# DeltaNet recurrence on Trainium2: five products as single heads in 64x64 tiles in place of stacked pairs of heads

## The chip, the cores and the metric

The kernel runs on one core of a Trainium2 chip. The metric is the device time of one execution in microseconds (us). Three runs of the kernel before took 383.0, 385.54 and 389.6 us; the median is 385.54. One execution more was taken with the hardware profiler.

## The reference

Two blocks follow one another. The first is a DeltaNet recurrence over 4 batches of 8 heads (32 heads in all), 768 tokens and a head dimension of 48. Cut to what matters:

```
k_n = k / (norm(k) + 1e-06)
for t in range(S):
    y[:, :, t] = einsum('bhd,bhde->bhe', q[:, :, t], state)
    v_old = einsum('bhde,bhd->bhe', state, kt)
    state = state + bt * einsum('bhd,bhe->bhde', kt, vt - v_old)
```

The output of the token comes from the state before the token's own update. The second block routes the 3,072 tokens (rows of 384 = 8 heads x 48) to one of 8 experts each by the largest logit, keeps the 80 tokens with the largest gate weight per expert, and runs a two-layer network (384 to 1,024 to 384, ReLU) on them. All other rows of the output are zero.

## The kernel before, in words

The recurrence is done in 12 chunks of 64 tokens. Inside a chunk the step-by-step update becomes matrix algebra: a unit triangular matrix of 64x64 per head is inverted, and products with it, with K, with Q and with the state S (48x48 per head) do the rest. A loop over `j` runs one stage per chunk. In stage j the chain for chunk j runs beside the preparation of later chunks.

All 32 heads are handled in each step. A head has three coordinates: `e` and `p` (0 or 1) and `g` (0 to 7). On chip, tensors with 64 rows per head hold two heads on 128 partitions, and which coordinate picks the half of the partitions depends on the tensor. All of this is in float32.

The products of stage j in TensorE's order are:

- `chain_ks`: K S, the state read with the chunk's keys, into the PSUM tile `a`. VectorE then forms R = V - K S.
- `logits` of chunk j-1 (24 small matmuls).
- `merge_f` of chunk j+1: the block B1 of the triangular matrix times the inverted 16x16 diagonal blocks that ScalarE has placed in `XB` (`place_x`). VectorE copies the result into `FB` under a mask.
- `chain_tr`: the inverse times R, into the tile `m2`. VectorE scales it by gam into `UB`.
- `chain_qs`: Q S, into `a`.
- `merge_y` of chunk j+1.
- `chain_ku`: K U, added into the state in PSUM, `S_ps`. ScalarE copies the state into `SB`.
- `chain_pu`: P U, added into `a` on top of Q S. ScalarE copies this output out (`x_out`), and a DMA writes it to `x_rows`.
- `merge_p` and `merge_u` of chunk j+1 in 32x32 tiles, with two Gram products of chunk j+5 between (`gram`), then transposes of the output (`out_t`).

Five of these (`chain_ks`, `chain_qs`, `chain_ku`, `chain_pu`, `merge_f`) take two heads in one matmul: two heads lie on the two halves of the 128 contraction rows, and the right side (`SB`, `UB`, `XB`) is stored block by block, with each head's data in one half of the columns and zeros in the other. So a product is 16 matmuls with 96 columns. `chain_tr` and `gram` instead take one head per matmul, on tiles of the array of 64 rows by 64 columns; the helper `tiles` deals the 32 matmuls out over four quadrants in turn. A helper `mm` records every matmul, so they all have line L231 in the profile.

The order of the work is written out by hand: each engine runs its instructions in the order in which the code emits them, and waits on semaphores for operands. The DMAs of the loop are issued by SP, also in order: `store` of B1 in eight small pieces, `load_v`, `fetch`, `load_kq`, in even stages `put` and `spread` (the inverted blocks, which POOL has solved, go out to memory and come back in another layout as XD and YD), `load_k`, zeroing of the output (`clear`), early weights (`load_first`), and `x_rows`. `fill` puts small VectorE steps of the gate between. From stage 7 on (`late`) there is no Gram product left, and `merge_p` comes ahead of `chain_pu`.

After stage 11 come the last gate steps, the choice of the 80 tokens, and the experts' network, which the change doesn't touch.

Of the kernel before, what the change touches and what calls it, by code (L numbers as in the profile page):

```python
# [32 lines left out]
def _layout(inputs):  # L33
# [13 lines left out]
    out["vtok"] = vb.transpose(4, 0, 5, 3, 1, 2, 6).reshape(NC, 128, 16 * D)  # L47
# [30 lines left out]
def kernel(  # L78
# [89 lines left out]
    with ExitStack() as actx:  # L168
# [19 lines left out]
        XB = blk.tile([128, NB, 2, 48], F32, name="XB")  # L188
        YB = blk.tile([128, NB, 2, 2, 16], F32, name="YB")
        FB = blk.tile([128, 2, 4, 2, 64], F32, name="FB")  # L190
        YF = fixed("YF", 2, [128, 2, 8, 64])
        PB_ = blk.tile([128, 2, 8, 32], F32, name="PB")
        SB = blk.tile([128, NQ, 2, 2, D], F32, name="SB")
        UB = blk.tile([128, NB, 2, D], F32, name="UB")
# [21 lines left out]
        PAIRS = [(a, 4 * c + ql) for a in range(2) for ql in range(4) for c in range(2)]  # L216
        XPAIRS = [(a, 4 * c + 2 * r + q) for a in range(2) for c in range(2) for q in range(2) for r in range(2)]

# [11 lines left out]
        def mm(out, lhsT, rhs, acc=False):  # L230
            nc.tensor.matmul(out, lhsT=lhsT, rhs=rhs, start=not acc, stop=not acc, skip_group_check=True)  # L231

# [51 lines left out]
        def norm_of(bs, ss):  # L284
# [22 lines left out]
            for i, c in enumerate(bs):  # L307
                for e in range(2):
                    for h in range(2):
                        nc.gpsimd.tensor_copy(nvs[hs(h), c, 8 * e : 8 * e + 8].rearrange("r (q p) -> r p q", p=2),  # L310
                                              nv[hs(e), i, :, h].rearrange("r (p q) -> r p q", p=2))
# [89 lines left out]
        def place_x(c, es=(0, 1)):  # L401
            if ok(c):
                for e in es:
                    for i in range(3):
                        nc.scalar.mul(XB[hs(e), :, e, 16 * i : 16 * i + 16], XD[hs(e), :, c % 2], bmask[hs(e), i : i + 1])  # L405

# [8 lines left out]
        def merge_f(c, ps):  # L415
            if ok(c):
                for p, g in PAIRS:
                    mm(ps[hs(g // 4), p, 96 * (g % 4) : 96 * (g % 4) + 96].rearrange("r (e w) -> r e w", e=2),
                       B1[c % B1n][:, slot(p, g)], XB[:, slot(p, g)])
                for p in range(2):  # L420
                    nc.vector.copy_predicated(FB[:, p].rearrange("r g e w -> r (g e) w")[:, :, 0:48],  # L421
                                              mask48.bitcast(I32).unsqueeze(1).to_broadcast([128, 8, 48]),
                                              ps[:, p, :384].rearrange("r (g w) -> r g w", w=48))

        def merge_y(c, ps):
            if ok(c):
                for m in range(8):
                    for e in range(2):
                        mm(ps[hs(e), 0, 64 * m : 64 * m + 64], FB[:, m // 4, m % 4, e], YB[:, 8 * e + m].rearrange("r h b w -> r (h b w)"))
# [5 lines left out]
        def merge_p(c, ps, eng=None):  # L435
            if ok(c):
                for m in range(8):
                    for e in range(2):
                        for h in range(2):
                            k = 64 * h + 32 * (m % 2)  # L440
                            mm(ps[k : k + 32, 1, 128 * e + 32 * (m // 2) : 128 * e + 32 * (m // 2) + 32],
                               FB[64 * h + 32 : 64 * h + 64, m // 4, m % 4, e, 0:32], YF[c % 2][64 * h + 32 : 64 * h + 64, e, m, 32:64])
# [7 lines left out]
        def merge_u(c, ps):  # L450
            if ok(c):
                for m in range(8):
                    for e in range(2):
                        for h in range(2):
                            k = 64 * h + 32 * (m % 2)
                            mm(ps[k : k + 32, 0, 128 * e + 32 * (m // 2) : 128 * e + 32 * (m // 2) + 32],
                               FB[64 * h : 64 * h + 32, m // 4, m % 4, e, 0:32], PB_[64 * h : 64 * h + 32, e, m])
# [6 lines left out]
        def chain_ks(c, ps):  # L464
            if ok(c) and c > 0:
                kq = KQ[c % KQn]
                for e, g in PAIRS:
                    mm(ps[hs(g // 4), e, 2 * D * (g % 4) : 2 * D * (g % 4) + 2 * D].rearrange("r (p d) -> r p d", p=2),
                       kq[:, g, 0, hs(e)], SB[:, g, e])
                for e in range(2):  # L470
                    nc.vector.tensor_tensor(out=R[:, 8 * e : 8 * e + 8], in0=VT[c % VTn][:, 8 * e : 8 * e + 8],  # L471
                                            in1=ps[:, e, : 8 * D].rearrange("r (g d) -> r g d", d=D), op=Alu.subtract)

        def chain_tr(c, ps):
            if ok(c):
# [3 lines left out]
                                         Y[hs(g // 4), e, pq(p, g)], r[hs(g // 4), 8 * e + 2 * (g % 4) + p]))  # L479
                for e in range(2):  # L480
                    bt = gam[hs(e), c].rearrange("r (g c) -> r c g", c=2).unsqueeze(3).to_broadcast([64, 2, 8, D])
                    nc.vector.tensor_tensor(out=UB[hs(e), :, e].rearrange("r (g c) d -> r c g d", c=2),  # L482
                                            in0=ps[hs(e), :, : 8 * D].rearrange("r c (g d) -> r c g d", d=D), in1=bt, op=Alu.mult)

        def chain_qs(c, ps):
            if ok(c) and c > 0:
                kq = KQ[c % KQn]
                for e, g in XPAIRS:
                    mm(ps[hs(g % 4 // 2), g // 4, 4 * D * (g % 2) : 4 * D * (g % 2) + 4 * D]
                       .rearrange("r (p e d) -> r e p d", p=2, e=2)[:, e], kq[:, g, 1, hs(e)], SB[:, g, e],  # L490
                       acc=e + g % 2 > 0)

        def chain_ku(c):
            if ok(c) and c < NC - 1:
                kb = KT[c % KTn]
                for g in range(NQ):
                    for p in range(2):
                        mm(S_ps[hs(p, D), g // 4, 2 * D * (g % 4) : 2 * D * (g % 4) + 2 * D].rearrange("r (e d) -> r e d", e=2),
                           kb[:, slot(p, g)], UB[:, slot(p, g)], acc=True)
                for p in range(2):  # L500
                    nc.scalar.copy(SB[hs(p, D), :, :, p].rearrange("r (b g) e d -> r b (g e) d", b=2),
                                   S_ps[hs(p, D), :, : 8 * D].rearrange("r b (g d) -> r b g d", d=D))

        def chain_pu(c, ps):
            if not ok(c):
                return
            for p, g in XPAIRS:
                o = 4 * D * (g % 2) + 2 * D * p
                mm(ps[hs(g % 4 // 2), g // 4, o : o + 2 * D].rearrange("r (e d) -> r e d", e=2), PT[c % PTn][:, slot(p, g)], UB[:, slot(p, g)],
                   acc=c > 0)  # L510

        def x_out(c, ps, b):
            if ok(c):
                nc.scalar.copy(x_t[c % 2][:, b].rearrange("r h d -> r (h d)"), ps[:, b, : 8 * D])
# [156 lines left out]
        for t in (YF[0], YF[1], XB, YB, SB, UB):  # L671
# [27 lines left out]
        nc.vector.tensor_copy(FB.rearrange("r p q e w -> r (p q e) w"), eye.unsqueeze(1).to_broadcast([128, NB, 64]))  # L699
# [63 lines left out]
        for j in range(NC):  # L763
# [19 lines left out]
            merge_f(j + 1, b2)  # L783
            chain_tr(j, m2)
            chain_qs(j, a)
            if j % 2:
                load_kq(j + 6)
            else:
                put([j + 2, j + 3])
                load_kq(j + 6, parts=(0,))  # L790
                spread(j + 2)
                load_kq(j + 6, parts=(1,))
# [5 lines left out]
            chain_ku(j)  # L798
            load_k(j + 8)
# [5 lines left out]
            late = not ok(j + 5)  # L805
            fill((4.5 if j > 7 else 4.5 if late else 4.0) - (1.9 if j == 0 else 2.9 if j % 2 and ok(j + 6) else 0))
            if late:
                merge_p(j + 1, b2)
            chain_pu(j, a)
# [228 lines left out]
```

## Time and profile before

| | |
|---|---|
| median of three runs | 385.54 us (383.0 to 389.6) |
| profiled execution, its own time | 381.74 us |
| its span | 380.0 us |
| granted TensorE clock over the span | 0.844 |
| TensorE matmul busy | 278.5 us, 73%, 7,337 records |
| VectorE, ScalarE, POOL busy | 200.0, 159.8, 149.8 us |
| before stage 0's T-product | 59.9 us |
| stage 0's T-product to stage 1's | 22.1 us |
| stage 1's T-product to stage 11's | 179.4 us |
| stage 11's T-product to the experts' network | some 51 us |
| experts' network | some 68 us |

In a windows answer each row is a stretch in us from the start of the span, with its length, the busy time of each engine and in brackets its number of instructions, then the clock that TensorE was granted (1.00 is full), the busy share of the DMA engines and their rate. In a groups answer a row is a line, an engine, an operation, what it writes and reads, shapes and count, then its busy time and the mean ns of one; after the next bar stands the idle time before it and what ended it. A waits row gives who waited for whom: us in total, how often, the longest. A timeline row gives the start, how long, engine, line, operation and count; in brackets stands the idle time ahead and what ended it. "PEld" is TensorE's weight load, "issue" a wait that nothing in the profile explains. Queue 1 carries SP's DMAs, queue 8 is one of those that the profile calls instruction queues.

### The profile page before, as it was taken

The page shows a single profiled execution, that of the slowest core. Times are in us where ns is not written, and L with a number is a line of the kernel's source. Part 1 is how long each engine was busy: PE and PEld are TensorE (multiplying, and loading weights), DVE is VectorE, ACT ScalarE, POOL GpSimd, SP SyncE. Part 2 cuts the span into 40 slices and gives each one's busy share as a digit, 9 for nine tenths or more (in the row PEclk, how much of TensorE's full clock was granted, in tenths as well). Part 3 has the DMA queues.
Part 4 walks back from the last instruction along what each step waited for, and adds up shares of the span by engine and source line. Part 5 has one row for each costly group of instructions (what it writes and reads, how often), then busy time and mean ns, then how long its engine had stood idle before and what let it go on. Part 6 is the DMA issues. An engine that isn't in the chain of part 4 may idle for free. (4 is left out here: it accounts for less than half of the span.)

```text
span 380.0 us, 16553 instructions
## 1 busy us (share of the span) xinstructions
PE 278.5 (73%) x7337; PEld 245.9 (65%) x7337; DVE 200.0 (53%) x489; ACT 159.8 (42%) x352; POOL 149.8 (39%) x375
## 2 busy tenths in 40 slices
PE   6334728666887988959997987697201699999994
PEld 2233528566786878949896977686101369999993
DVE  4599826427334969664457467576897710010001
ACT  3202567357557575765667577771200001211120
POOL 7375138715861586068607860100610061011001
PEclk9855778969699998897988599999755558999998
DMA  8786864487267745753658059818799942661000
GB/s 308 194 330 201 86 194 111 128 191 238 42 194 175 239 90 142 155 196 68 155 158 283 4 119 343 304 63 270 256 428 427 422 144 59 253 252 38 17 17 26
DMA packets 75879, 69.52 MB, mean 183 GB/s; under 512 B 57248, under 2 KB 65440, under 8 KB 73504
## 3 DMA queue, kind: packets, MB, share of 16 engines
q1 hardware_dynamic: 70080, 65.03, 54.7%
q10 hardware_dynamic: 4960, 1.48, 1.8%
q0 software_dynamic: 768, 1.97, 1.8%
q8 instruction: 57, 0.93, 1.0%
q14 instruction: 14, 0.11, 0.1%
HBM read 53.32 MB, written 15.14 MB: 180 GB/s over the span
## 5 line engine op out<-in xcount | busy, mean ns | idle before, releaser
L231 PE MATMUL pm<-KQ 48*64 48x128 f32 x704 | 29.3, 315 | 27.1 <-DMA KQ<-in_kqt_dram 14.0
L231 PE MATMUL pm<-SB,KQ 128*64 128x96 f32 x704 | 39.3, 273 | 5.0 <-ACT YF L461 4.9
L231 PEld LDWEIGHTS pm<-KQ 48*64 48x64 f32 x704 | 23.9, 157 | 29.3 <-DVE XY L375 11.9
L231 PEld LDWEIGHTS pm<-SB,KQ 128*64 128x64 f32 x704 | 35.0, 155 | 8.7 <-ACT YF L461 6.8
L316 POOL TENSOR_TENSOR VT<-VT,nvs 128x768 f32<-128x768 f32 x12 | 17.7, 1475 | 51.6 <-DMA VT<-in_vtok_dram 36.6
L405 ACT ACTIVATE XB<-XD,cst 64x256 f32<-64x256 f32 x72 | 31.2, 495 | 7.6 <-DMA XD<-inv_blocks 7.2
L999 ACT ACTIVATE hT<-hp 128x320 f32<-128x320 f32 x16 | 7.0, 437 | 64.8 <-PE hp L996 64.8
L373 POOL TENSOR_TENSOR tmpTrue<-XY,NT 128x28 f32<-128x28 f32 (+13 forms) x84 | 30.8, 367 | 6.1
L231 PE MATMUL pm<-XB,B 128*64 128x96 f32 x384 | 22.3, 279 | 14.4 <-ACT XB L405 14.4
L432 ACT COPY YF<-pm 64x256 f32<-64x256 f32 x48 | 17.6, 367 | 35.8 <-PE pm L231 35.4
L967 DVE COPY xTe<-xp 128x240 f32<-128x240 f32 x8 | 3.3, 408 | 52.7 <-PE xp L965 52.7
L375 POOL TENSOR_TENSOR XY<-XY,tmpTrue 128x28 f32<-128x28 f32 (+13 forms) x84 | 28.0, 334 | 6.6
L231 PEld LDWEIGHTS pm<-XB,B 128*64 128x64 f32 x384 | 19.8, 160 | 15.5 <-ACT XB L405 15.1
L1007 PE MATMUL yp<-hT,w 128*64 128x80 f32 x768 | 28.8, 234 | 0.3 <-issue 0.3
L981 POOL DMA_INDIRECT out_dram<-y,idx_s x8 | 7.3, 918 | 54.3 <-DVE y L980 54.3
L421 DVE COPY_PREDICATED FB<-cst,pm 128x384 f32<-128x384 int32 x24 | 12.8, 588 | 30.2 <-PE pm L231 30.2
L1007 PEld LDWEIGHTS yp<-hT,w 128*64 128x64 f32 x768 | 27.3, 137 | 1.8 <-ACT hT L999 1.1
L332 DVE TENSOR_TENSOR B<-pm,ngam 128x512 f32<-128x512 f32 x22 | 15.1, 690 | 19.8 <-PE pm L231 19.2
L482 DVE TENSOR_TENSOR UB<-pm,gam 64x768 f32<-64x768 f32 x24 | 22.9, 955 | 4.2 <-PE pm L231 3.7
L471 DVE TENSOR_TENSOR R<-VT,pm 128x384 f32<-128x384 f32 x22 | 11.2, 551 | 21.7 <-PE pm L231 11.0
L411 ACT ACTIVATE YB<-YD,cst 64x256 f32<-64x256 f32 x48 | 21.7, 498 | 0.5
L956 POOL DMA_INDIRECT xg<-x_rows,idx_g x8 | 7.5, 938 | 30.5 <-DVE idx_s L939 28.4
(175 smaller groups left out, 609.0 us busy)
## 6 DMA issues: line engine op xcount, KB each, us to landing
w<-in_w_dram SPq DMA_DIRECT2D x12, 1536.0 KB, 14.6
KQ<-in_kqt_dram SPq DMA_DIRECT2D x6, 1024.0 KB, 7.3
KQ<-in_kqt_dram SPq DMA_DIRECT2D x12, 512.0 KB, 5.8
KQ<-in_w_dram SPq DMA_DIRECT2D x12, 512.0 KB, 6.4
VT<-in_vtok_dram SPq DMA_DIRECT2D x12, 384.0 KB, 4.2
x_rows<-x SPq DMA_DIRECT2D x12, 384.0 KB, 4.6
out_dram<-zero SPq DMA_DIRECT2D x12, 384.0 KB, 4.5
KT<-in_ktok_dram SPq DMA_DIRECT2D x11, 384.0 KB, 7.8
```

What stands on the lines that cost most here:

```text
L231: nc.tensor.matmul(out, lhsT=lhsT, rhs=rhs, start=not acc, stop=not acc, skip_group_check=True)
L316: eng.tensor_tensor(out=V, in0=V, in1=nvs[:, c].unsqueeze(2).to_broadcast([128, NB, D]), op=Alu.mult)
L332: nc.vector.tensor_tensor(out=own(B1[c % B1n], h), in0=pv[:, 0], in1=own(ngam[:, c].unsqueeze(2).to_broadcast([128, NB, 64]), h), op=Alu.mult)
L373: eng.tensor_tensor(out=tv, in0=X[:, :, t + 1 :, t : t + 1].to_broadcast(sh), in1=NT[:, :, 0:t, t].unsqueeze(2).to_broadcast(sh), op=Alu.mult)
L375: eng.tensor_tensor(out=X[:, :, t + 1 :, 0:t], in0=X[:, :, t + 1 :, 0:t], in1=tv, op=Alu.add)
L405: nc.scalar.mul(XB[hs(e), :, e, 16 * i : 16 * i + 16], XD[hs(e), :, c % 2], bmask[hs(e), i : i + 1])
L411: nc.scalar.mul(YB[hs(h), :, h, b], YD[hs(h), :, c % 2], bmask[hs(h), 2 * b + 1 : 2 * b + 2])
L421: nc.vector.copy_predicated(FB[:, p].rearrange("r g e w -> r (g e) w")[:, :, 0:48], mask48.bitcast(I32).unsqueeze(1).to_broadcast([128, 8, ...
L432: nc.scalar.copy(YF[c % 2][hs(h), e].rearrange("r m (b x w) -> r m b x w", b=2, x=2)[:, :, :, 1], ps[hs(e), 0].rearrange("r (m h b w) -> r ...
L471: nc.vector.tensor_tensor(out=R[:, 8 * e : 8 * e + 8], in0=VT[c % VTn][:, 8 * e : 8 * e + 8], in1=ps[:, e, : 8 * D].rearrange("r (g d) -> ...
L482: nc.vector.tensor_tensor(out=UB[hs(e), :, e].rearrange("r (g c) d -> r c g d", c=2), in0=ps[hs(e), :, : 8 * D].rearrange("r c (g d) -> r ...
L1007: nc.tensor.matmul(yp[r, d * cap : (d + 1) * cap], lhsT=w2_t[f][:, d * 128 + 64 * n : d * 128 + 64 * n + 64], rhs=hT[:, f, :], start=(f == ...
```

## The change

Five products become single heads on 64x64 tiles over four quadrants, as `chain_tr` already is, and their right sides become dense: `XB`, `UB` and `SB` lose the axis that held zeros, and `SB` is doubled. The number of matmuls in each goes from 16 to 32, the columns from 96 to 48. The heads in `VT`, `R` and `FB` are ordered anew so that the copies and VectorE's operations take whole halves of PSUM. `place_x` takes all 128 partitions at once, three instructions for six. `UB` is scaled in two instructions of 128 partitions in place of two of 64. Q S is done in two parts: half of the heads ahead of `chain_tr`, half after `chain_pu`[...]. `load_kq`, `load_k`, `clear` and `load_first` move behind the second part; `put` and `spread` move behind `chain_ku`. Three fills with zeros at the start go away.

```diff
-        XB = blk.tile([128, NB, 2, 48], F32, name="XB")
+        XB = blk.tile([128, NB, 48], F32, name="XB")
-        FB = blk.tile([128, 2, 4, 2, 64], F32, name="FB")
+        FB = blk.tile([128, 2, 8, 64], F32, name="FB")
-        SB = blk.tile([128, NQ, 2, 2, D], F32, name="SB")
-        UB = blk.tile([128, NB, 2, D], F32, name="UB")
+        SB = fixed("SB", 2, [128, 2, NQ, D])
+        UB = blk.tile([128, NB, D], F32, name="UB")
...
+        def xmm(row, ps, ops, acc, heads=HEADS):
+
+            seen = set()
+
+            def emit(e, p, g):
+                t = g % 4 // 2, e
+                o = D * (4 * (g // 4) + 2 * (g % 2) + p)
+                mm(ps[hs(t[0]), e, o : o + D], *ops(e, p, g), acc=acc or t in seen)
+                seen.add(t)
+
+            tiles(lambda e, p, g: (row(e, p), g % 4 // 2), emit, heads)
...
-        def place_x(c, es=(0, 1)):
-            if ok(c):
-                for e in es:
-                    for i in range(3):
-                        nc.scalar.mul(XB[hs(e), :, e, 16 * i : 16 * i + 16], XD[hs(e), :, c % 2], bmask[hs(e), i : i + 1])
+        def place_x(c):
+            if ok(c):
+                for i in range(3):
+                    nc.scalar.mul(XB[:, :, 16 * i : 16 * i + 16], XD[:, :, c % 2], bmask[:, i : i + 1])
...
-                for p, g in PAIRS:
-                    mm(ps[hs(g // 4), p, 96 * (g % 4) : 96 * (g % 4) + 96].rearrange("r (e w) -> r e w", e=2),
-                       B1[c % B1n][:, slot(p, g)], XB[:, slot(p, g)])
+                tiles(lambda e, p, g: (e, g // 4),
+                      lambda e, p, g: mm(ps[hs(g // 4), e, 48 * pq(p, g) : 48 * pq(p, g) + 48],
+                                         B1[c % B1n][hs(e), slot(p, g)], XB[hs(e), slot(p, g)]))
...
-                for e, g in PAIRS:
-                    mm(ps[hs(g // 4), e, 2 * D * (g % 4) : 2 * D * (g % 4) + 2 * D].rearrange("r (p d) -> r p d", p=2),
-                       kq[:, g, 0, hs(e)], SB[:, g, e])
+                tiles(lambda e, p, g: (p, g // 4),
+                      lambda e, p, g: mm(ps[hs(g // 4), p, D * (2 * (g % 4) + e) : D * (2 * (g % 4) + e) + D],
+                                         kq[hs(p, D), g, 0, hs(e)], SB[c % 2][hs(p, D), e, g]))
...
-                for e in range(2):
-                    bt = gam[hs(e), c].rearrange("r (g c) -> r c g", c=2).unsqueeze(3).to_broadcast([64, 2, 8, D])
-                    nc.vector.tensor_tensor(out=UB[hs(e), :, e].rearrange("r (g c) d -> r c g d", c=2),
-                                            in0=ps[hs(e), :, : 8 * D].rearrange("r c (g d) -> r c g d", d=D), in1=bt, op=Alu.mult)
+                for h in range(2):
+                    bt = own(gam[:, c].unsqueeze(2), h).to_broadcast([128, 8, D])
+                    nc.vector.tensor_tensor(out=own(UB, h), in0=ps[:, h, : 8 * D].rearrange("r (m d) -> r m d", d=D), in1=bt, op=Alu.mult)
...
-        def chain_qs(c, ps):
+        def chain_qs(c, ps, k):
...
-                for e, g in XPAIRS:
-                    mm(ps[hs(g % 4 // 2), g // 4, 4 * D * (g % 2) : 4 * D * (g % 2) + 4 * D]
-                       .rearrange("r (p e d) -> r e p d", p=2, e=2)[:, e], kq[:, g, 1, hs(e)], SB[:, g, e],
-                       acc=e + g % 2 > 0)
+                xmm(lambda e, p: p, ps, lambda e, p, g: (kq[hs(p, D), g, 1, hs(e)], SB[c % 2][hs(p, D), e, g]), k > 0,
+                    [hd for hd in HEADS if hd[0] ^ hd[1] != k])
...
-                for g in range(NQ):
-                    for p in range(2):
-                        mm(S_ps[hs(p, D), g // 4, 2 * D * (g % 4) : 2 * D * (g % 4) + 2 * D].rearrange("r (e d) -> r e d", e=2),
-                           kb[:, slot(p, g)], UB[:, slot(p, g)], acc=True)
-                for p in range(2):
-                    nc.scalar.copy(SB[hs(p, D), :, :, p].rearrange("r (b g) e d -> r b (g e) d", b=2),
-                                   S_ps[hs(p, D), :, : 8 * D].rearrange("r b (g d) -> r b g d", d=D))
+                tiles(lambda e, p, g: (e, p),
+                      lambda e, p, g: mm(S_ps[hs(p, D), e, D * g : D * g + D], kb[hs(e), slot(p, g)], UB[hs(e), slot(p, g)], acc=True))
+                for e in range(2):
+                    nc.scalar.copy(SB[(c + 1) % 2][:, e].rearrange("r g d -> r (g d)"), S_ps[:, e, : 8 * D])
...
-            for p, g in XPAIRS:
-                o = 4 * D * (g % 2) + 2 * D * p
-                mm(ps[hs(g % 4 // 2), g // 4, o : o + 2 * D].rearrange("r (e d) -> r e d", e=2), PT[c % PTn][:, slot(p, g)], UB[:, slot(p, g)],
-                   acc=c > 0)
+            xmm(lambda e, p: e, ps, lambda e, p, g: (PT[c % PTn][hs(e), slot(p, g)], UB[hs(e), slot(p, g)]), c > 0)
...
-        for t in (YF[0], YF[1], XB, YB, SB, UB):
+        for t in (YF[0], YF[1], YB):
...
+            chain_qs(j, a, 0)
             chain_tr(j, m2)
-            chain_qs(j, a)
-            if j % 2:
-                load_kq(j + 6)
-            else:
-                put([j + 2, j + 3])
-                load_kq(j + 6, parts=(0,))
-                spread(j + 2)
-                load_kq(j + 6, parts=(1,))
             merge_y(j + 1, b2)
...
             chain_ku(j)
+            if j % 2 == 0:
+                put([j + 2, j + 3])
+                spread(j + 2)
...
             chain_pu(j, a)
+            chain_qs(j, a, 1)
+            load_kq(j + 6)
             load_k(j + 8)
...
-                place_x(j + 2, (0,))
+                place_x(j + 2)
                 out_t(j, m2)
-                place_x(j + 2, (1,))
```

## The prediction

> **What bounds the kernel now.** I read the windows cut at the start of each stage's T-product first, then the groups by shape, then the waits, then the TensorE timeline of one stage, and last the queues. Two full stages, as the windows show them:
>
> ```profile
> core 0: us, PE busy (x) PEld busy (x) DVE busy (x) ACT busy (x) POOL busy (x), PEclk, DMA share, GB/s
> ...
> 103.70:121.70 18.00, 14.29 (x483) 13.30 (x481) 7.40 (x13) 11.36 (x26) 7.72 (x18) 1.00 0.78 196
> 121.70:139.20 17.50, 14.76 (x484) 13.33 (x482) 12.62 (x23) 12.10 (x28) 11.35 (x26) 1.00 0.53 150
> ```
>
> TensorE is busy over 80% of a stage and every other engine well under; the recurrence (stages 1 to 10, 82.0 to 261.4 us) takes 179.4 us, and TensorE is what most of it waits on. But 3.2 us per stage are not TensorE work. The waits name two kinds that matter:
>
> ```profile
> PEld pm L231 <- ACT XB L405: 15.1, 7, 6.4
> ...
> PEld pm L231 <- issue: 14.5, 21, 3.8
> ```
>
> The first is merge_f waiting for ScalarE's placed blocks. The second says "issue": TensorE stood still and no semaphore explains it. The timeline of stage 2 shows one such place, and the prices of the products:
>
> ```profile
> 103.69 1.15 PE L231 MATMUL pm<-R,YF 64*64 64x48 f32 x64
> 104.77 1.54 PE L231 MATMUL pm<-SB,KQ 128*64 128x96 f32 x32
> 106.14 1.10 PE L231 MATMUL pm<-YB,FB 128*64 128x64 f32 x32
> 107.07 1.49 PE L231 MATMUL S_ps<-UB,KT 128*48 128x96 f32 x32
> 108.39 1.49 PE L231 MATMUL pm<-UB,PT 128*64 128x96 f32 x32
> 109.81 0.81 PE L231 MATMUL pm<-YF,FB 32*32 32x32 f32 x64
> 112.10 1.10 PE L231 MATMUL pm<-KQ 48*64 48x128 f32 x32 [1.48 <-issue]
> ```
>
> See that one f32 product is two matmul records (16 written, 32 recorded), and that the Gram product at 112.10 lost 1.48 us to "issue". What it waited for is in the queue table:
>
> ```profile
> q8 instruction: 57, 0.93, 1.0%
> ```
>
> 57 packets of 16 KB are 0.93 MB; 7,337 matmuls and 7,337 weight loads are 14,674 instructions, so 64 B each and 256 to a packet: queue 8 is TensorE's own program. I set the start of each packet in the trace's DMA records beside the running count of matmuls. The stops lie about 255 counted instructions apart or at multiples of that, and TensorE goes on 1.2 to 1.6 us after the packet has landed: packet landed 94.76, on at 96.12; 110.53 and 112.10; 114.66 and 115.94; 163.94 and 165.32; 169.05 and 170.55. There are 11 such stops, 14.7 us. All fit one rule: the packet for block k+1 is asked for when TensorE enters block k, and TensorE waits at the end of k if it isn't there. From entering a block to the next being usable (packet end plus 1.37 us) took, over 35 blocks, 2.5 us at the tenth of the way, 3.65 at the median, 5.3 at nine tenths, 3.86 in the mean: the packet takes about 1.0, and the rest is its delay, zero when the DMA engines are idle, up to 4.6 us behind a KQ load.
>
> **What the Trainium skill says.** "Runtime: NRT & Kernel Launch", Instruction fetch mechanics: programs stream in 16 KiB blocks of 256 instructions, the next fetched while the current one runs. The trace agrees. The page also gives TensorE room for 2,048 instructions and calls the cost mostly hidden; here TensorE behaves as with two blocks, and the cost is 14.7 us. "DMA: Bandwidth & Descriptors", Queues, rings and completion order: an engine goes round its queues packet by packet, so a fetch waits behind data; this fits the delays. "TensorE: Matmul & The Clock Gate", Part 3: products in different tiles of rows and columns run concurrently; the T-product agrees, 64 records in 1.08 us, 17 ns each. "TensorEngine Tiling (Array Packing)", Gotcha 1: different row tiles can't use one PSUM bank at once, which is why Q S must go in two parts; no run here shows what a collision costs.
>
> **The change part by part.**
>
> *The five products.* Start to start at full clock, from the timeline: XB 1.45, K S and Q S 1.37 each, K U 1.32, P U 1.42, together 6.93 us a stage. The form they take (64 records of 64x64 with 48 columns) is that of the T-product, 1.08 us, so 5.40 after (Q S as two halves of 0.54). Gain 1.53 us a stage of TensorE time, 15.3 in ten stages. K and Q have 48 rows of contraction and K U 48 output columns, which the T-product doesn't; I bound them by 0.9 to 1.3 us and take 1.08.
>
> *Their instructions.* Each product goes from 16 to 32 matmuls, each of two passes with a weight load: 64 more instructions, 320 a stage. A full stage has 484 matmuls now, 968 instructions or 3.8 blocks; it gets 1,288 or 5.05. From 82.0 to 261.4 there are 4,502 matmuls, 9,004 instructions, 35.3 blocks of 5.1 us; with 3,200 more, 47.9 blocks.
>
> *ScalarE.* The XB placement goes from six instructions to three of twice the partitions (the 128-partition YF placement L413 takes 501 ns, the 64-partition one 495): 1.3 us a stage less by the spacing. The state copy goes from two of 48x768 (793 ns) to two of 128x384 (480, as x_out's L514): 0.6 us less. In even stages the XB queue behind xT is what merge_f waits for, 0.35 to 1.27 us; I take 4 us in all as gained.
>
> *VectorE.* UB goes from two of 955 ns to two of 128x384, as R's 551: 0.8 us less. UB was hidden behind Q S and Y B (1.37 + 0.93); the part of Q S left there has moved ahead of T, and Y B alone (0.93) must hide it. The first UB (0.15 + 0.55 after T) is in time, and K U's first half needs only it; the second (1.25) is needed at 0.93 + 0.54. No cost, 0.3 us a stage if the order inside slips.
>
> *Q S in two parts.* The first now writes where K S's result stands and so waits for R. Behind that wait stands T, which needs R anyway; after K S come logits 0.75 and merge_f 1.08, against R's 0.15 + 1.02. No cost. The second part delays x_out by 0.54 us; in full stages PB, behind it on ScalarE, gets this back from the shorter state copy. In late stages PB is ahead of x_out.
>
> *Moved DMAs.* In even stages put and spread now stand behind K U in the program, but SP only waits for POOL and earlier DMAs there, so they start when they did; spread no longer queues behind half of the KQ load, up to 1 us sooner. The KQ load (1 MB), KT, the zeroing and the weight loads behind it on SP come after P U and Q S: 3 to 5 us later in odd stages. Gram needs the KQ load 15 us or more later, so no wait; but these transfers now lie beside the Y F, Gram and P B products (384 instructions in 3.6 us), where blocks are shortest. Three POOL memsets of 1.38 us go from the start, where POOL waits for VectorE's norms anyway: nothing.
>
> *The sum.* Without the fetch, TensorE's time between stops is 179.4 - 14.7 = 164.7; less 15.3 and 4 leaves 145.4 over 47.9 blocks, 3.0 us a block where 4.7 stood. Now a block lasts as long as the longer of its work and its fetch. I pair the observed lengths without stops (2.4, 3.4, 4.2, 5.4, 8.7 us at the quarters) with all 35 fetch times: the mean of the larger is 5.14, and 5.13 was measured, so the rule holds for before. With the same lengths scaled to a mean of 3.0 it is 4.17: three blocks in four are shorter than the mean fetch. 47.9 x 4.17 = 200 us, against 179.4: 20 us slower. If fetches are delayed 10% less, because the same data spreads over a longer time, it is 4.04, and 14 us. I take the middle and the small gain at stage 0 with it: 16 us. The profiled execution, 381.7 us with a span of 380.0, would be 397.7, a factor of 1.042; it lies below all three timed runs, so on the median of 385.5 this is 401.
>
> **The rivals.** *Fetch hidden, faster.* The mechanism is the fetch's delay behind data, at every block from 82 to 261 us: if moving the KQ load frees it, and a fetch takes about 2.8 us, the same pairing gives 3.35 a block, 160 us, a gain of 19. The loop of store, fetch, POOL solve, put and spread limits this: in stages 1 to 6 a pair of stages can't fall under some 35 us, since placed blocks already start within 0 to 3 us of their data. So 14 us gained, 371. For it speak the gain in each engine's time and blocks of 2.4 us that passed at 68 us; against it, that a fetch under 3 us was had in one block of four only. The sign turns at a mean fetch of 3.3 us; a gain over 2% needs 3.1. *They cancel.* Mean fetch 3.4 to 3.6: 0 to 8 us slower, 386 to 393. *Clock as well.* The granted clock was 0.79 to 0.84 in four stages with stops; with more stops the Y F to K S part would run cold: 8 to 15 us more, 410 to 417. *The quadrants don't overlap.* Excluded in the main by the T-product; at 1.37 a product nothing is gained, and the forecast rises by 7.
>
> **How the numbers follow.** Slower through the fetch, 0.62, with the clock, 0.07; cancelled, 0.17; faster, 0.14. Two per cent is about what a measurement of this kernel tells from no change: 377.8 to 393.3. The slower cases put 0.68 above it, the cancelled case and the edges 0.18 inside, 0.14 below. The range leaves out the faster case and the worst of the clock: 378 to 417.
>
> **What would show it.** Queue 8 with some 70 packets in place of 57; "issue" waits of TensorE at 40 us or more in place of 14.5; the five products at 1.08 us where no stop falls inside; XB waits under 8 us; stages of 19 to 20 us with TensorE busy two thirds. I am wrong if the packets are many and the stops few: then fetches run further ahead than I read, or the moved loads delay them less.

## The result

The changed kernel takes 423.78 us (median of four runs, 421.19 to 425.63) where the kernel before takes 384.27 (four runs, 378.62 to 389.6). The ratio is 1.1124, with a 95% interval of 1.0975 to 1.1272: 11% slower. The prediction had said slower, by 16 us; it was 39.5, and the time lies outside the range of 378 to 417. The profiled execution took 421.19 us with a span of 419.5, so 39.5 us more than that of before (380.0). Each kernel has faster and slower executions; the ratios here and below compare the fast ones with fast runs of the kernel before taken in the same series, so they can differ a little from a quotient of two medians.

The queue table and the clock over 40 slices, on the page of the changed kernel:

```profile
PEclk9755857685666657587977598658555565999998
...
q8 instruction: 72, 1.18, 1.2%
```

The clock row of the kernel before:

```profile
PEclk9855778969699998897988599999755558999998
```

TensorE's program now comes in 72 packets in place of 57, as foreseen (some 70). The middle of the clock row (slices 8 to 29) is mostly fives to eights where before it was mostly nines and eights.

The windows, cut at the T-product (`chain_tr`) of stages 2, 3 and 4, and then from stage 1's to stage 11's:

```profile
108.18:130.22 22.04, 18.90 (x646) 17.17 (x646) 6.68 (x15) 9.68 (x23) 6.88 (x14) 0.65 0.62 159
130.22:154.72 24.50, 19.25 (x647) 17.55 (x646) 10.93 (x25) 10.05 (x24) 16.22 (x44) 0.64 0.38 106
81.74:297.66 215.92, 167.38 (x6073) 151.64 (x6072) 96.01 (x237) 94.19 (x225) 84.37 (x202) 0.70 0.52 148
```

The last stretch in the kernel before:

```profile
82.00:261.40 179.40, 150.31 (x4502) 137.71 (x4500) 110.44 (x237) 113.73 (x251) 84.67 (x202) 0.90 0.60 169
```

This stretch grew by 36.5 us, so nearly the whole loss is in it. ScalarE and VectorE have less to do, as meant (94 for 114 us, 96 for 110), and that bought nothing. TensorE is busy for longer, 167 for 150 us, although each new product is cheaper at full clock: the clock fell from 0.90 to 0.70. The DMA engines are less busy, 0.52 for 0.60.

The waits of TensorE's weight loads in the changed kernel:

```profile
PEld pm L228 <- issue: 40.4, 31, 3.9
...
PEld pm L228 <- ACT XB L412: 7.7, 7, 3.3
```

"issue" has gone from 14.5 to 40.4 us, from 21 times to 31; the wait for the placed blocks from 15.1 to 7.7. (Most of that wait falls before stage 1: within the stretch it went from 4.1 to 1.5 us.) The timeline of stage 3 shows the stops and what the products cost:

```profile
130.22 1.92 PE L228 MATMUL pm<-R,YF 64*64 64x48 f32 x64
132.08 1.38 PE L228 MATMUL pm<-YB,FB 128*64 128x64 f32 x32
133.38 0.60 PE L228 MATMUL S_ps<-UB,KT 64*48 64x48 f32 x33
135.22 0.53 PE L228 MATMUL S_ps<-UB,KT 64*48 64x48 f32 x28 [1.23 <-issue]
...
135.60 1.06 PE L228 MATMUL pm<-UB,PT 64*64 64x48 f32 x60
...
139.22 0.99 PE L228 MATMUL pm<-YF,FB 32*32 32x32 f32 x63 [1.89 <-issue]
140.14 1.99 PE L228 MATMUL pm<-KQ 48*64 48x128 f32 x32
142.06 0.68 PE L228 MATMUL pm<-PB,FB 32*32 32x32 f32 x33
144.87 0.67 PE L228 MATMUL pm<-PB,FB 32*32 32x32 f32 x31 [2.13 <-issue]
...
148.85 1.96 PE L228 MATMUL pm<-SB,KQ 48*64 48x48 f32 x64
```

There are three stops in 15 us. In the trace's DMA records the packets before them landed at 133.83, 137.65 and 143.50; TensorE goes on 1.39, 1.57 and 1.37 us later. Where TensorE runs, it is often cold, that is, at half of its clock: the P U product at 135.60 takes 1.06 us, the K S product at 148.85, with as many matmuls of 48 columns, 1.96. The T-product, which the change leaves alone, takes 1.92 us or more in nine of the stages 1 to 11; in the kernel before it took 1.15 in seven of them. By the groups, the prices taken for the other engines held:

```profile
L412 ACT ACTIVATE XB<-XD,cst 128x256 f32<-128x256 f32 x36 | 15.7, 498 | 4.9 <-DMA XD<-inv_blocks 4.7
...
L488 DVE TENSOR_TENSOR UB<-pm,gam 128x384 f32<-128x384 f32 x24 | 12.3, 553 | 21.7 <-PE pm L228 21.7
...
L502 ACT COPY SB<-S_ps 128x384 f32<-128x384 f32 x22 | 9.5, 482 | 4.3 <-PE S_ps L228 4.2
```

Set block by block, as the prediction did for before (a block is 256 instructions; its fetch runs from entering the block to 1.37 us after the next packet's end):

| stage 1's T to stage 11's | before | after |
|---|---|---|
| stops for the fetch | 12, 15.4 us | 30, 43.4 us |
| mean length of a block | 5.03 us | 4.54 us |
| TensorE's time of a block, without stops | 4.61 us | 3.63 us |
| mean time of a fetch | 4.0 us | 4.19 us |
| fetches at 10, 50, 90% | 2.80, 3.74, 5.31 us | 3.19, 3.94, 5.92 us |

This count finds 12 stops in the kernel before and a mean fetch of 4.0 us, where the prediction's own count had 11 and 3.86. By the table, 28 of the 36.5 us are stops. The rest, 8.5 us, is TensorE's time between the stops: 164.0 us before and 172.5 now, where the prediction had it fall to 145.4. The 47 fetches add up to 197 us. Had they stayed as long as they were, even a TensorE that took no time for the products would have needed more than the 179.4 us of before.

### The profile page after: what moved, and what is told of

The parts are those of the page before. It is cut to its first block, busy times and chain, and to the rows that moved or that the text cites. A ratio compares the mean times of both kernels' runs of the same rounds, so it can differ in the third digit from the quotient of the medians.

```text
span 419.5 us, 20152 instructions
## 1 busy us (share of the span) xinstructions
PE 300.1 (72%) x9161; PEld 264.0 (63%) x9161; DVE 183.2 (44%) x489; ACT 135.4 (32%) x316; POOL 145.7 (35%) x372
## 5 line engine op out<-in xcount | busy, mean ns | idle before, releaser
L228 PE MATMUL pm<-SB,KQ 48*64 48x48 f32 x1408 | 39.0, 268 | 2.6 <-ACT YF L467 1.9
L228 PEld LDWEIGHTS pm<-SB,KQ 48*64 48x64 f32 x1408 | 35.0, 184 | 6.7 <-ACT YF L467 2.9
L340 DVE TENSOR_TENSOR B<-pm,ngam 128x512 f32<-128x512 f32 x22 | 15.1, 689 | 35.3 <-PE pm L228 25.1
L228 PE MATMUL pm<-PB,FB 32*32 32x32 f32 x768 | 14.7, 232 | 15.5 <-issue 11.8
L228 PE MATMUL pm<-XB,B 64*64 64x48 f32 x768 | 20.3, 277 | 6.1 <-ACT XB L412 5.9
L228 PE MATMUL pm<-R,YF 64*64 64x48 f32 x704 | 19.9, 288 | 5.5 <-issue 5.5
L228 PEld LDWEIGHTS pm<-PB,FB 32*32 32x32 f32 x768 | 12.3, 140 | 18.1 <-issue 13.6
L228 PE MATMUL pm<-YF,FB 32*32 32x32 f32 x768 | 11.9, 201 | 16.0 <-issue 12.9
L228 PEld LDWEIGHTS pm<-XB,B 64*64 64x64 f32 x768 | 18.5, 192 | 7.2 <-ACT XB L412 6.4
L228 PEld LDWEIGHTS pm<-R,YF 64*64 64x64 f32 x704 | 18.9, 207 | 5.8 <-issue 5.8
L467 DVE COPY YF<-pm 32x256 f32<-32x256 f32 x24 | 9.9, 414 | 28.9 <-PE pm L228 28.7
## 6 DMA issues: line engine op xcount, KB each, us to landing
w<-in_w_dram SPq DMA_DIRECT2D x12, 1536.0 KB, 14.8
```

The lines of the kernel that those rows point to most:

```text
L340: nc.vector.tensor_tensor(out=own(B1[c % B1n], h), in0=pv[:, 0], in1=own(ngam[:, c].unsqueeze(2).to_broadcast([128, NB, 64]), h), op=Alu.mult)
L467: (nc.scalar.copy if h else nc.vector.tensor_copy)(YF[c % 2][64 * h : 64 * h + 32].rearrange("r e (m x) w -> r e m x w", x=2)[:, :, :, x, ...
```

## The experiments

The theory is that the number of TensorE's instructions sets the loss, through the fetch of the program. The rivals are that the loss comes from the form (quadrants), from the transfers that moved, or from the cold clock.

**1. The number of matmuls alone, in the kernel before.** The five products stay stacked on 128 rows, but each matmul of 96 columns becomes two of 48. There are no quadrants and no moved transfers.

```diff
-                for e, g in PAIRS:
-                    mm(ps[hs(g // 4), e, 2 * D * (g % 4) : 2 * D * (g % 4) + 2 * D].rearrange("r (p d) -> r p d", p=2),
-                       kq[:, g, 0, hs(e)], SB[:, g, e])
+                halves(PAIRS, lambda n, e, g: mm(ps[hs(g // 4), e, 2 * D * (g % 4) + D * n : 2 * D * (g % 4) + D * n + D],
+                                                 kq[:, g, 0, hs(e)], SB[:, g, e, n]))
...
```

> The kernel before, each of the five stacked products issued as 32 matmuls of 48 columns in place of 16 of 96: same tiles, same arithmetic, same order of everything else, 320 more TensorE instructions a stage. Theory (TensorE waits for its program, then runs cold): some 70 packets in queue 8, 25 to 45 us of unexplained stops where the kernel before has 15, mean granted clock under 0.78, 405 to 440 us. Rival 1 (the quadrant form itself runs slowly or lowers the clock): no quadrants are added here, so 380 to 390 us. Rival 2 (the moved transfers): nothing is moved, 380 to 390 us.

Measured: 419.4 us, ratio 1.0972 (1.0892 to 1.1051). The recurrence in the windows, the wait, and one product in the timeline:

```profile
83.69:300.36 216.67, 184.75 (x6066) 171.49 (x6064) 107.67 (x237) 114.03 (x251) 84.64 (x202) 0.85 0.49 138
```

```profile
PEld pm L237 <- issue: 25.6, 24, 2.4
```

```profile
158.05 2.03 PE L237 MATMUL pm<-UB,PT 128*64 128x48 f32 x63
```

The time is what the theory gave, but the reason is only in part its own. The clock was 0.85 in the stretch (0.82 over the span), not under the expected 0.78. A stacked product of 64 records takes 2.0 us, not the 1.37 of 32, so five products in ten stages cost some 32 us of TensorE's own time (184.8 busy for 150.3); counted block by block, the stops grew by only some 7 to 9 us. The run shows that neither quadrants nor moved transfers are needed for a loss of this size. It doesn't show that the stops make it.

**2. The changed kernel with half of the matmuls.** Each product becomes 16 matmuls of 96 columns on the same quadrants, with everything else as changed. Half of the left sides are left out: a head's right side is multiplied by its neighbour's left side, so the numbers computed are other ones.

```diff
-                       lambda e, p, g: mm(ps[hs(g // 4), p, D * (2 * (g % 4) + e) : D * (2 * (g % 4) + e) + D],
-                                          kq[hs(p, D), g, 0, hs(e)], SB[c % 2][hs(p, D), e, g]))
+                       lambda e, p, g: mm(ps[hs(g // 4), p, D * (2 * (g % 4) + e) : D * (2 * (g % 4) + e) + 2 * D].rearrange("r (n d) -> r n d", n=2),
+                                          kq[hs(p, D), g, 0, hs(e)], SB[c % 2][hs(p, D), :, g]),
+                       [hd for hd in HEADS if hd[0] == 0])
...
```

> The changed kernel with 16 matmuls of 96 columns on the four quadrants in each of the five products, in place of 32 of 48: one head's left side is used for two heads' right sides, so half of the left sides are left out; every other instruction, the layouts and the order of transfers stay. TensorE's instructions are back at the number of the kernel before. Theory: 57 packets in queue 8, stops of 8 to 18 us, clock 0.85 or more, the products at 0.8 to 1.1 us each at full clock, 345 to 375 us. Rival 1 (quadrants lower the clock): clock stays near 0.72 and the time over 400 us. Rival 2 (moved transfers): over 400 us.

Measured: 379.67 us, ratio to before 0.9886 (0.9834 to 0.9939), with 57 packets on queue 8. The windows and three products in the timeline (the profiled execution took 383.24 us):

```profile
79.95:260.13 180.18, 141.04 (x4504) 124.46 (x4500) 95.65 (x237) 95.52 (x228) 84.50 (x202) 0.76 0.62 173
```

```profile
179.01 0.88 PE L228 MATMUL S_ps<-UB,KT 64*48 64x96 f32 x32
179.71 0.84 PE L228 MATMUL pm<-UB,PT 64*64 64x96 f32 x32
180.37 0.51 PE L228 MATMUL pm<-SB,KQ 48*64 48x96 f32 x16
```

Going from 32 matmuls to 16 takes 44 us off the changed kernel, with its quadrants, its dense operands and its moved transfers all in place. That clears the form and the moved transfers as the cause of the loss. It doesn't divide the loss: the stops fall by 24 us against the changed kernel, and TensorE's busy time by 26. The expectation of 345 to 375 was missed by 5 us; the stops (15, 19.8 us) are a little above the 8 to 18 expected, and the clock of 0.76 is well under the 0.85. From start to start a product takes some 0.7 us here at full clock, for 1.37 before, 34 us in ten stages by the timeline, and almost none of that shows in the time. The low clock takes part of it back: TensorE's busy time falls by 9 us only, from 150 to 141. Part goes into waits: in the stretch TensorE's weight loads wait 9.7 us for the placed blocks (4.1 in the kernel before), and ScalarE, which places them, sits idle for 9.5 us until their data arrive.

**3. The moved transfers alone, in the kernel before.**

```diff
-            if j % 2:
-                load_kq(j + 6)
-            else:
-                put([j + 2, j + 3])
-                load_kq(j + 6, parts=(0,))
-                spread(j + 2)
-                load_kq(j + 6, parts=(1,))
...
+            if j % 2 == 0:
+                put([j + 2, j + 3])
+                spread(j + 2)
...
             chain_pu(j, a)
+            load_kq(j + 6)
...
```

> The kernel before with the changed kernel's order of transfers alone: the KQ and KT loads, the zeroing and the early weights behind P U, put and spread behind K U. Theory: within 2% of the kernel before, 378 to 392 us, 57 packets in queue 8, stops of 10 to 22 us. Rival 2 (the moved transfers delay TensorE's program or the recurrence's data): 395 to 420 us, stops of 25 us or more.

Measured: 388.5 us, ratio 1.0151 (1.0072 to 1.0229). Windows and wait:

```profile
84.47:271.26 186.79, 151.62 (x4499) 138.99 (x4497) 107.46 (x237) 113.98 (x251) 84.36 (x202) 0.89 0.59 163
```

```profile
PEld pm L231 <- ACT XB L405: 22.9, 6, 6.8
PEld pm L231 <- issue: 17.0, 21, 3.0
```

A small loss of some 6 us (3 to 9 by the interval) is real, where the prediction had put the moved transfers at nothing. "issue" is 2.5 us above before. The rest shows in the wait for the placed blocks: 22.9 us for 15.1, and within the stretch 11.5 for 4.1, as much as the stretch grew (7.4 us). In two stages ScalarE itself sat idle for the data of these blocks, 6.8 us in all, which it never did in this stretch before. Which of the moved transfers delays them isn't shown. In the changed kernel the wait within the stretch is 1.5 us, so this loss is no visible part of its 39 us.

**4. The changed kernel with a warmer clock.** Eight matmuls of 512 columns in bf16 are added per stage, into a tile that is overwritten later.

```diff
+            heat(8, m2)
```

> The changed kernel with 8 matmuls of 512 bf16 columns (16 instructions, 1.7 us at full clock, 3.4 at half) added in each stage behind the second part of Q S; their result is used by nothing. If the low clock is a loss of its own that follows from TensorE standing still, and the added work fills the time in which the next block of program is on its way: clock 0.82 or more, Y F to K S products back from 1.9 to 1.1 us, 395 to 420 us. If the clock doesn't answer to the activity, or the stops are all that counts: 12 x 1.7 to 3.4 us on top, 435 to 465 us, clock near 0.72.

Measured: 421.91 us, ratio to before 1.0967 (1.0817 to 1.1117; the changed kernel itself 1.1124). Windows, and the added work in the timeline:

```profile
82.83:298.24 215.41, 162.69 (x6149) 136.49 (x6146) 95.37 (x237) 94.18 (x224) 84.63 (x202) 0.86 0.52 147
```

```profile
203.91 1.90 PE L643 MATMUL pm<-ones_b 128*128 128x512 bf16 x8
```

The clock rose from 0.70 to 0.86, as expected, and the time missed the expected 395 to 420 us by 2. TensorE's time of a block stayed at 3.61 us (3.63): the added 1.9 us a stage took the place of the time that the warmer clock saved. Without the added work, TensorE was busy for some 144 us of the stretch in place of 167. So this run moves the clock and not the time, and doesn't show what a warm clock would be worth alone. An estimate of the most that it could be worth comes from the blocks of the changed kernel: where no stop falls, they exceed their own fetch by 16.8 us in all. If the fetches stay as long, a clock of 1.00 saves no more than that, and some 20 of the 36.5 us remain.

**5. and 6. Both kernels with less data to carry.** The loads of K and Q from chunk 6 on, of the transposed K from chunk 8 on, the zeroing of the output and the experts' early weights are left out, in the changed kernel and in the kernel before. All instructions of the products stay; they compute with old data.

```diff
-            nc.sync.dma_start(t[:, k], w1[e, :, c * F : c * F + F])
...
-            if ok(c):
+            if 0 <= c < KTn:
...
-            if ok(c):
+            if 0 <= c < KQn:
...
-            if a < zr.shape[0]:
+            if a < 0:
...
```

> The changed kernel without the KQ loads from chunk 6 on, the KT loads from chunk 8 on, the zeroing of the output and the early weights (some 18 MB left out; the chunks and the experts compute on what lies in the buffers). TensorE's program and all other instructions stay. Theory (the blocks of TensorE's program queue behind data): stops in the recurrence fall from 43 to 20 to 32 us, the mean time to get a block from 4.2 to 3.4 to 3.8 us, the stretch from stage 1's to stage 11's T-product from 216 to 190 to 203 us. Rival (the stops are TensorE's own rate or follow from the clock, not from the data): stops 38 to 48 us, the stretch 210 to 220 us.

> The kernel before with the same transfers left out. Theory: stops in the recurrence fall from 15 to under 8 us, the stretch from stage 1's to stage 11's T-product from 179 to 163 to 174 us, less than the changed kernel gains. Rival (data not the cause): stops 12 to 18 us, the stretch 176 to 183 us.

Measured: the changed kernel 403.87 us, ratio to before 1.0652 (1.0471 to 1.0833); the kernel before 370.3, ratio 0.9766 (0.9627 to 0.9905). The windows of the changed kernel with less data, then of the kernel before with less data, and the wait of the latter:

```profile
81.49:278.41 196.92, 162.02 (x6072) 147.14 (x6072) 98.50 (x237) 94.27 (x225) 83.01 (x201) 0.72 0.30 72
```

```profile
81.92:246.48 164.56, 141.49 (x4498) 128.83 (x4496) 112.10 (x237) 113.57 (x251) 83.08 (x201) 0.97 0.35 85
```

```profile
PEld pm L230 <- issue: 1.6, 5, 0.8
```

With the DMA share down to 0.30, the mean fetch of the changed kernel falls from 4.19 to 3.70 us and its stops from 43.4 to 28.4; the stretch shrinks by 19 us. In the kernel before, the stops all but vanish and the stretch shrinks by 14.8. Both expectations were met. So part of the mean fetch is delay behind data, and the greater part isn't: the changed kernel still stops 26 times, and without most of its data it is still slower than the kernel before with all of it.

**7. The rate at which TensorE's program arrives, by itself.** At the end of the kernel before, where the DMA engines are idle, some 4,000 matmuls are issued with no wait between them: `seg` takes their number, rows, columns of the array, columns of the right side, and the places on the array.

```diff
...
+    seg(1024, 64, 64, 48, q4)
+    seg(512, 64, 64, 96, q4)
+    seg(512, 128, 64, 96, ((0, 0), (0, 64)))
+    seg(1024, 128, 64, 48, ((0, 0), (0, 64)))
+    seg(1024, 64, 64, 48, q4)
```

> The kernel before with five runs of matmuls behind its last result, where no data moves and nothing is waited for: 1,024 on 64x64 quadrants with 48 columns, 512 on quadrants with 96 columns, 512 stacked (128 rows, 64 columns of the array) with 96, 1,024 stacked with 48, and 1,024 quadrants with 48 again. Theory (a block of 256 instructions can't come faster than every 3.4 to 3.8 us even with the DMA engines idle): the first and last take 54 to 61 us each (16 blocks), the second 27 to 31 us, the third 44 us (its own rate, 43 ns a record), the fourth 54 to 66 us. Rival (the program comes as fast as the T-product runs, and only data delays it): first and last 35 us, second 23 us, third 44 us, fourth 44 to 66 us.

Measured in one execution of 621.15 us. The timeline, in single heads on quadrants (48 columns, the form of the change), then on quadrants with 96 columns:

```profile
403.91 2.08 PE L1020 MATMUL hp<-cst 64*64 64x48 f32 x128 [1.39 <-issue]
407.38 2.08 PE L1020 MATMUL hp<-cst 64*64 64x48 f32 x128 [1.39 <-issue]
411.40 2.08 PE L1020 MATMUL hp<-cst 64*64 64x48 f32 x128 [1.94 <-issue]
...
435.97 2.87 PE L1020 MATMUL hp<-cst 64*64 64x96 f32 x128 [0.60 <-issue]
439.44 2.87 PE L1020 MATMUL hp<-cst 64*64 64x96 f32 x128 [0.60 <-issue]
```

The windows of the 48-column quadrants, of stacked pairs with 96 columns, and of stacked pairs with 48:

```profile
378.54:432.50 53.96, 31.33 (x1920) 29.41 (x1921) 0.00 (x0) 0.00 (x0) 0.00 (x0) 1.00 0.02 6
471.73:503.68 31.95, 31.95 (x787) 31.95 (x783) 0.00 (x0) 0.00 (x0) 0.00 (x0) 1.00 0.01 3
514.86:560.10 45.24, 45.24 (x1559) 45.24 (x1556) 0.00 (x0) 0.00 (x0) 0.00 (x0) 1.00 0.02 4
```

This is the plainest view of the cause, and the times are those of the theory, not of its rival (35 us for the first stretch). No engine but TensorE works, nothing is moved but the program (DMA share 0.02), the clock is at 1.00, and TensorE stops after every 128 records, which are 256 instructions. 15 blocks take 53.96 us, 3.60 each, of which 2.08 are work. With twice the columns the work is 2.87 us, and the usual period is the same 3.47. The DMA records give the parts of the usual period: 1.13 us from going on to the start of the next packet, 1.0 for the packet, 1.36 from its end to the next instruction, 3.5 together. So in this run block after block of 256 instructions comes no faster than every 3.5 us, 3.6 in the mean or 14 ns an instruction. A float32 product of 32 matmuls is 128 instructions, so at this rate it can't be sustained below 1.8 us, whatever the T-product does in 1.08 between two stops. Stacked pairs with 96 columns take 31.95 us / 787 = 40.6 ns a record and never stop. With 48 columns they take 29.0 ns, 3.71 us a block, just above the period. The last stretch, quadrants with 48 columns again, stops as the first does.

**8. One product changed.** The kernel before with `merge_f` alone in the new form, with the dense `XB`.

```diff
-                for p, g in PAIRS:
-                    mm(ps[hs(g // 4), p, 96 * (g % 4) : 96 * (g % 4) + 96].rearrange("r (e w) -> r e w", e=2),
-                       B1[c % B1n][:, slot(p, g)], XB[:, slot(p, g)])
+                tiles(lambda e, p, g: (e, g // 4),
+                      lambda e, p, g: mm(ps[hs(g // 4), e, 48 * pq(p, g) : 48 * pq(p, g) + 48],
+                                         B1[c % B1n][hs(e), slot(p, g)], XB[hs(e), slot(p, g)]))
...
```

> The kernel before with merge_f alone in the new form: 32 matmuls of 48 columns on four quadrants, dense XB, three placements for six; order of transfers, chain products and their layouts as before. 64 more instructions a stage, a fifth of the change. Theory: stops 18 to 26 us; ScalarE's 1.3 us and TensorE's 0.4 us a stage about pay for them: 378 to 392 us. Rival (any product on quadrants is a gain by itself and only the sum of all is too much): 368 to 377 us. Rival (the loss goes by product, a fifth of 40 us each): 388 to 396 us.

Measured: 387.45 us, ratio 1.0242 (1.0105 to 1.0379), 60 packets, 14 stops of 23.2 us. The windows:

```profile
81.92:264.85 182.93, 147.82 (x4793) 135.72 (x4789) 105.86 (x237) 102.07 (x226) 84.49 (x202) 0.91 0.60 167
```

A fifth of the added matmuls already costs 1 to 4%, though ScalarE has 11.6 us less to do in the stretch (102.1 for 113.7) and no transfer is moved. The gain on ScalarE, which was the best reason for the change, doesn't pay for 3 packets. That quadrants are a gain by themselves (368 to 377 us) is excluded. Whether the loss goes by product, a fifth of 40 us each, isn't told apart from the theory: the stretch of the profiled execution is 3.5 us longer, the ratio says some 9.

**9. and 10. Less data in front of the fetches.** First, the kernel before loads only the 48 rows of each 64 of K and Q that are used, from chunk 6 on. Second, on top of this, four of the five early loads of the experts' weights come after the recurrence.

```diff
-                        eng.dma_start(dst[:, p * w : p * w + w], kqt[c, :, p * w : p * w + w])
+                        for h in range(2):
+                            eng.dma_start(dst[hs(h, D), p * w : p * w + w], kqt[c, hs(h, D), p * w : p * w + w])
```

```diff
...
-                if j > NC - KQn:
-                    load_first(j - 1 - NC + KQn)
+                if j == NC - KQn + 1:
+                    load_first(0)
...
-        load_first(KQn - 1)
         for k in range(WR):
+            if k + 1 < KQn:
+                load_first(k + 1)
             load_w(k)
...
```

> The kernel before, with the KQ loads from chunk 6 on bringing only the 48 rows in use of each 64 (the others hold zeros from the first loads already): 1.5 MB less, twice as many issues on SP, same result. Theory (data ahead of TensorE's program costs time): 1 to 4 us less than the kernel before, stops 10 to 14 us. Rival (the number of issues and SP's order count, not the bytes): 0 to 4 us more.

> The same, and the early weights of slots 1 to 4 (4 MB) loaded behind the recurrence between the other weights in place of stages 8 to 11. Theory: stops in stages 8 to 11 fall by 1 to 3 us; the experts' network starts as before, since its first weights still come first: 2 to 6 us less than the kernel before. Rival (the memory is full between 266 and 304 us, so the experts wait for weights): 3 to 12 us more.

Measured: 381.97 us, ratio 0.9973 (0.994 to 1.0006), with stops of 12.7 us (15.4); and 383.72, ratio 1.0028 (0.9998 to 1.0058). Neither makes a measurable difference. The first expected 1 to 4 us less and got 1, which its rival (0 to 4 us more) isn't told apart from by an interval of 2.3 less to 0.2 more; the second missed its 2 to 6 us less. The 14.8 us that the sixth run gained by leaving the data out aren't had by moving a part of it.

## Why the prediction was off

The direction and the mechanism of the stops were right: there are more packets and more stops, and the other engines were relieved for nothing. Two terms of its sum were too small, and one choice. The larger error is in TensorE's time between the stops: 145.4 us were foreseen, 172.5 were measured.

**The fetch.** "3.86 in the mean", with the packet at 1.0 and the rest its delay, "zero when the DMA engines are idle". It was 4.19 (4.0 in the kernel before, counted the same way). The seventh run shows the error in that split: with idle DMA engines a fetch still takes 3.5 us, because 1.13 us pass before the packet starts. The fetches under 3 us in the stretch of before had their packet start between 1.05 us ahead of the block's first recorded matmul and 0.49 us after it, and none of these blocks was entered after a stop; after a stop the packet never started sooner than 1.04 us. When TensorE keeps stopping, this head start is gone. So the lower part of the distribution moved up (2.80 to 3.19 us at a tenth), and the fetches got longer although the DMA share fell. Pairing TensorE's time of 3.0 us a block with the fetches of after gives 4.41 us in place of 4.17 to 4.23 with those of before; over 47.9 blocks that is 9 to 11 us.

**TensorE's time of a block.** "3.0 us a block"; it was 3.63. The products do take about 1.06 us at full clock, as at 135.60, but many ran cold, at up to 1.96. The prediction took the clock as a rival of its own, with 8 to 15 us at a chance of 0.07, and should have had it in the main sum. With 3.63 and the fetches of after the pairing gives 4.60 a block, 9 us more; 4.54 was measured. The shares depend on the order: put in first, with the fetches of before, TensorE's time is worth some 12 us, and the fetches the rest. For the clock's part in it there is an estimate. In the fourth run, at a clock of 0.86 in place of 0.70, a block took 3.2 us without the added work (3.61 less 18.7 us over 47 blocks), so some 0.4 of the 0.63 us go with the clock. What lowers the clock stays open.

**The choice of 16 us.** The sum gave 20, and 14 with fetches delayed 10% less; the middle was taken. The delay didn't fall, so 4 us of this were wrong too. That "issue" came to the 40 us foreseen is in part luck: the sum itself held some 54 us of stops (200 less 145.4), and the longer work between the stops hid some of what the longer fetches added.

**The smaller terms.** The wait for the placed blocks fell below 8 us (7.7); but of the 15.1 us read as a wait that matters, only 4.1 lay in the recurrence, and 2.6 of them were gained, not 4. The other engines' prices held, and no cost of Q S in two parts or of the memsets was seen. The moved transfers cost about 6 us in the kernel before, not nothing. Stages of 19 to 20 us were foreseen; they took 17.2 to 26.4, 21.6 in the mean, and TensorE was busy 78% rather than two thirds, since cold work counts as busy. (The first of the two stages that it read as busy over 80% is at 79%.)

**The rivals.** "Fetch hidden" needed a mean fetch of 3.1 us; the seventh run shows that not even idle DMA engines give it where every block ends in a stop. "They cancel" needed 3.4 to 3.6, which is the floor itself. "Clock as well" (410 to 417) was nearest, and still short.

## What to carry to other kernels

Count TensorE's instructions before making its products smaller: a float32 matmul is four of them here, and where blocks of 256 followed one another with a stop after each, every block took some 3.5 us or more, however little work it held. (Single blocks that TensorE entered without a stop passed faster.) The price of a product that is read from a few records between two stops isn't one that can be sustained; multiply it by the number of products per block of instructions and see whether the block lasts as long as its fetch. A wait called "issue" that recurs at a fixed count of instructions, together with packets on an instruction queue, points to this limit.

## What the runs showed beyond that

- The Trainium skill, "Runtime: NRT & Kernel Launch", Instruction fetch mechanics, says that fetching is hidden because issuing is slower than filling. For these products the seventh run shows the reverse: 8.1 ns an instruction inside a block (2.08 us / 256), 14 ns with the stops. A remark of the same section that only two blocks of the program are held fits: in the quadrant stretches every stop lies one block after the last.
- A stacked product isn't halved by halving its columns: 40.6 ns a record at 96 columns, 29.0 at 48. On quadrants it is 22 ns at 96 (2.87 us / 128) and 16 at 48.
- The clock isn't explained by the idle time alone. The stretch had 34.9 us of TensorE idle in the fifth run at a clock of 0.72, and 35.2 in the third at 0.89. The kernels with all five products on quadrants ran at 0.70 to 0.76 (0.86 with the added work of the fourth run), those with stacked ones at 0.85 to 0.97; yet quadrants in the seventh run, which began at full clock, kept 1.00 through a stop of 1.4 us in every 3.5. What pulls it down in the recurrence stays open.
